# A round trip through DRAM in a Fourier and soft-MoE kernel: the transposing step moved from the reads to the stores, three weight tiles loaded earlier

## The chip, the cores and the metric

The kernel runs on one core of one Trainium2 chip, with its five engines: TensorE (PE), VectorE (DVE), ScalarE (ACT), GpSimd (POOL) and SyncE (SP), which issues nearly all transfers, in a fixed order. The metric is the device time of one execution in microseconds; lower is better.

## What is computed

The input x has 8 batches of 2,496 tokens with 256 channels. The first half is a spectral layer, the second a soft mixture of 8 experts with 4 slots each:

```python
X = rfft(x, axis=1)
Yr = Xr @ w_r - Xi @ w_i + b_r ; Yi = Xr @ w_i + Xi @ w_r + b_i
Y = softshrink(Yr, 0.01) + 1j * softshrink(Yi, 0.01)
x = irfft(Y).reshape(19968, 256)

logits = x @ phi                       # 32 columns
d = softmax(logits over all tokens)    # per slot
slot_out[e] = relu((d.T @ x)[e] @ w1[e]) @ w2[e]
c = softmax(logits over the 32 slots)  # per token
out = c @ slot_out
```

## The kernel before, in words

A transform of length 2,496 is done as 39 x 64: with `f1` over 39 points, then over 64. The token index is split so that each half is a matrix product on TensorE; between the halves the data has to be regrouped from "one partition per (position, frequency k)" to "one partition per position of the other factor", and this goes through DRAM. `a_unit` (L322) does the first half of a batch, writes its result `ast` to DRAM as `adr` and `load_ap` (L383) reads it back as `ap`. A step (`steps`, five per batch, four frequencies each) then does the second half (`f2`: px), the complex linear layer in split precision (`lin_k`: pk; `lin_y`: py), the shrinking (`rt`), the 32 logit columns of the spectrum (`tp_p`: pq, collected per batch as `p_sb`) and a transposed copy of the spectrum (`tp_t`: pt, T).

When the five steps of a batch are through, `c_stages` (L604) runs that batch's chain on the logits, beside the steps of the next batch: `p_sb` times `sinv` (pg) gives `g_sb`, the inverse transform over 64; `g_sb` is stored in DRAM as `gd`, read back as `gp` in another grouping, and `gp` times `m2` (pL) gives the logits `L` of the batch's tokens. From `L` follow the running maximum, the exponentials `ee`, a forward transform of them (`ea`, stored as `ed`, read back as `eb`), and the sums pr of the slots. `halves` (L578) splits each operand into a high and a low part: ScalarE casts `chpL` from `gp`, VectorE subtracts to get `clpL`, and three products make one. For batch 6 the operands are used unsplit. Batch 7 has no next batch: `last_chain` (L924) runs it in the tail, with `g_sb` stored in three parts (frequencies 0 to 11, 12 to 15, 16 to 19) as they come. Then the experts (hps, po) and the output (pq, ost, out).

Shapes of the regrouping: `g_sb` has 128 partitions, 2 parts c (real, imaginary) x 64 positions n, each with 20 frequencies k x 32 columns s. `gp` has 120 partitions, 3 groups r x 40 (c, k), each with 22 positions g x 32. Position n is 22r + g for the groups 0 and 1 and for g under 20 in group 2; its last two columns repeat positions 44 and 45, the first two of the same group.

The order of work is written out by hand. Each generator (`c_stages`, `a_unit`, `load_w` by `at` and so on) yields times of a made-up clock; a heap (`run_until`) records the instructions in the order of these times, and `_InOrder`, `sp`, `aq`, `mm` keep that order on every engine. A step is 4 units long, and TB = 166 is the time at which the steps end. The table `PLAN` holds the times: `pg`, `pL` and so on for the chain, `wl` for the 32 weight tiles (0.5 MB each, counted from TB, with a letter for the place: r, a, x and T reuse tiles of the chain or of the steps, x and T as two halves; t lies in a pool of NTA tiles, the second number of `nw`, that takes the place of the first half's buffers; h in a pool of the tail). The helper lines that the profile shows are L177 (all VectorE, ScalarE and GpSimd work), L234 (SP's transfers), L240 (products) and L530 (transposes).

Of the kernel before, what the change touches and what calls it, by code (L numbers as in the profile page):

```python
# [11 lines left out]
F32 = mybir.dt.float32  # L12
# [37 lines left out]
def _constants():  # L50
    n1 = np.arange(N1)
    k1 = np.arange(K1)
    a39 = 2 * np.pi * (np.outer(n1, k1) % N1) / N1
    c39, s39 = np.cos(a39), np.sin(a39)
    s39[:, 0] = 0.0
    a64 = 2 * np.pi * (np.outer(np.arange(N2), np.arange(N2)) % N2) / N2
    q = np.outer(np.arange(N2), np.arange(N2)) % N2
    c64, s64 = np.cos(a64), np.sin(a64)
    c64[(q == 16) | (q == 48)] = 0.0
    s64[(q == 0) | (q == 32)] = 0.0  # L60

    f1 = np.zeros((R, N1, R, 2, K1))
    m2 = np.zeros((R, 2, K1, R, N1))
    wk = np.where(k1 == 0, 1.0, 2.0) / N
    for r in range(R):
        f1[r, :, r, 0] = c39
        f1[r, :, r, 1] = -s39
        m2[r, 0, :, r] = (c39 * wk).T
        m2[r, 1, :, r] = (-s39 * wk).T
    f1 = f1.reshape(P1, Q1)  # L70
    m2 = m2.reshape(Q1, P1)

    suni = np.zeros((2, N2, 2, N2))
# [14 lines left out]
    smov = smov.reshape(128, K1 + 1, 64)
    smov = np.concatenate([smov[:, : KG + 1], smov[:, :1], smov[:, KG + 1 :]], axis=1).reshape(128, -1)
    sinv = suni[np.arange(128).reshape(2, N2).T.reshape(-1)].T  # L90
    sgn = np.ones((2, N2, K1))
    sgn[1] = sig.T
    sgn = sgn.reshape(128, K1)
    dsc = sgn * wk[None, :]

    ident = np.eye(128)
    dmask = np.tile(np.eye(32), (4, 4))
    f1a = f1.reshape(P1, R, 2, NGRP, KG).transpose(0, 3, 2, 4, 1).reshape(P1, Q1)
    f1 = f1.reshape(P1, R, 2 * K1).transpose(0, 2, 1).reshape(P1, Q1)
# [12 lines left out]
    return {k: np.ascontiguousarray(v.astype(np.float32)) for k, v in out.items()}
# [27 lines left out]
    "to": 0.7,  # L140
    "ws": [-29, -28.9, -28.8, 2],
    "late": {'6': {'cms': [19.75, 19.71, 860.75, 862, 864, 865], 'pd': [20.36, 20.37], 'pr': [31.55, 31.6, 31.65, 31.7, 31.75], 'pL': [5.4, 5.8], 'pm': 6.875, 'pb': 7.325, 'pe': [8.75, 9.75], 'pg': [0.875, 1.275], 'fr': {'sinv': 0, 'm2': 0, 'f1': 0, 'suni': 0}}, '5': {'pg': [1.1, 1.8], 'pL': [4.95, 5.75], 'pm': 6.8, 'pb': 7.15, 'pe': [9.2, 9.9], 'pd': [13.8, 14.8], 'pr': [15.0, 17.25, 19.5, 21.75, 24.0]}, '4': {'pr': [18.4, 20.49, 24.49, 28.49, 32.49]}},
    "T_": {'wl': [[-45, 'r'], [-44, 'r'], [-43, 'r'], [-31.0, 't'], [-30.7, 't'], [-29.4, 't'], [-27.6, 't'], [-27.8, 't'], [-11, 'a'], [-10.3, 'a'], [-9.6, 'a'], [-7.5, 'x'], [-6.4, 'x'], [1.11, 'x'], [1.07, 'h'], [1.08, 'h'], [1.09, 'h'], [1.1, 'h'], [1.11, 'h'], [13.55, 'h'], [13.1, 'h'], [13.6, 'h'], [13.6, 'h'], [13.61, 't'], [13.61, 't'], [13.61, 't'], [13.61, 't'], [13.61, 't'], [13.7, 'T'], [13.7, 'T'], [13.7, 'T'], [13.7, 'T']], 'cl': 16, 'cp': 46.5, 'ct': 46.6, 'du': [[-4.5, 0], [-2.4, 0], [1.2, 0]], 'd1': [5, 2, 4, 0, 0, 0], 'cm': [19.9, 19.91, 19.92, 25, 25.1, 25.2], 'cm7': [18, 20, 22, 23, 25, 27], 'ye': 0.2, 'te': [[5.6, 0.2], [5.5, 0.4]], 'pg': [-7, -3.25, -0.35], 'yt': 0.5, 'wr': -30.6, 'tp': [0, 0.9, 1.05, 0.5], 'tt': [[-0.4, 0.5, 0.6, 0.7, 0.8], [12, 12.1, 12.2, 12.3, 12.4]], 'z': 13.55, 'th': [0.1, 0.12], 'tl': [0.2, 0.25]},
    "f1": [1.5, 2.15],
    "kw": [[-40, 9]],
    "ap1": 1.85,
    "f0": 0.2,
    "nw": [3, 10, 9],
    "te": 'A',
    "tp": [0.5, 1.0, 1.9, 1.8],  # L150
    "tt": [2, 2.5],
# [29 lines left out]
def fourier_soft_moe_kernel(ctx: ExitStack, tc: tile.TileContext, t: dict, out: bass.AP):  # L181
# [396 lines left out]
    def halves(n, t0, times, out, const, fr, src, evac):  # L578
# [13 lines left out]
        for h in range(2):  # L592
# [8 lines left out]
            yield t0 + times[h] + 0.25  # L601
            evac(h, out[1](ps))

    def c_stages(b):  # L604
        ct_ = "ps"
        K_ = dict(PLAN, **PLAN["late"].get(str(b), {}))
# [8 lines left out]
            lambda h, ps: A.copy(out=g_sb[:, h * 10 : h * 10 + 10, :].rearrange("p k s -> p (k s)"), in_=ps),  # L615
        )
        yield t0 + K_["pg"][1] + 0.35
        gd = dr.tile([N2, 2 * K1, S], F32, tag="gd", name=f"gd{b}")
        sp(out=gd.rearrange("n (c k) s -> (n c) k s", c=2), in_=g_sb)
        yield t0 + K_["pg"][1] + 0.9  # L620
        gp = wtile([Q1, G, S], F32, "gp", f"gp{b}")
        for r in range(R):
            ge = 22 if r < 2 else 20
            p0 = r * 2 * K1
            sp(
                out=gp[p0 : p0 + 2 * K1, :ge, :],
                in_=gd[22 * r : 22 * r + ge].rearrange("g k s -> k g s"),
            )
# [295 lines left out]
    def last_chain():  # L924
        b = B - 1
        for (k0, k1), tk in zip(((0, 12), (12, 16), (16, 20)), T_["pg"]):
# [12 lines left out]
        for r in range(R):
            ge = 22 if r < 2 else 20  # L940
            p0 = r * 2 * K1
            sp(
                out=gp[p0 : p0 + 2 * K1, :ge, :],
                in_=gd[22 * r : 22 * r + ge].rearrange("g k s -> k g s"),
            )
            if ge < G:
                sp(
                    out=gp[p0 : p0 + 2 * K1, ge:, :],
                    in_=gd[22 * r : 22 * r + G - ge].rearrange("g k s -> k g s"),
                )  # L950
# [310 lines left out]
```

## Time and profile before

| | |
|---|---|
| median of 3 runs | 580.69 us (577.52 to 581.72) |
| profiled execution | 575.19 us, of which the span from first to last instruction is 573.4 us |
| mean granted TensorE clock | 0.971 |
| chain that ended last, by engine | PE 65%, DMA 14%, DVE 12%, ACT 3% |
| of it, DMA gp<-gd and gd<-g_sb | 3% and 3% |
| TensorE, VectorE, ScalarE, GpSimd busy | 92%, 73%, 52%, 49% |
| DMA moved | 118.55 MB, mean 207 GB/s |

How to read it: a timeline row has the start in us, the time that it took, engine, line, operation, tiles (out<-in), shape and how often; in brackets, how long the engine stood idle before and what ended that. SPq is SP's queue: such a row is the issue of a transfer, not the transfer. A row of the chain of waits has start, length and what it was; there a DMA is shown from the issue to the landing that somebody waited for. A row of the table of stretches has, per engine, busy us and instructions, then the granted TensorE clock, the mean busy share of the 16 DMA engines, and what they moved.

### The profile page before, as it was taken

The page shows a single profiled execution, that of the slowest core. Times are in us where ns is not written, and L with a number is a line of the kernel's source. Part 1 is how long each engine was busy: PE and PEld are TensorE (multiplying, and loading weights), DVE is VectorE, ACT ScalarE, POOL GpSimd, SP SyncE. Part 2 cuts the span into 40 slices and gives each one's busy share as a digit, 9 for nine tenths or more (in the row PEclk, how much of TensorE's full clock was granted, in tenths as well). Part 3 has the DMA queues.
Part 4 walks back from the last instruction along what each step waited for, and adds up shares of the span by engine and source line. Part 5 has one row for each costly group of instructions (what it writes and reads, how often), then busy time and mean ns, then how long its engine had stood idle before and what let it go on. Part 6 is the DMA issues. An engine that isn't in the chain of part 4 may idle for free.

```text
span 573.4 us, 11788 instructions
## 1 busy us (share of the span) xinstructions
PE 528.8 (92%) x4358; PEld 447.4 (78%) x4358; DVE 419.3 (73%) x837; ACT 298.6 (52%) x650; POOL 281.0 (49%) x258
## 2 busy tenths in 40 slices
PE   8668999999999999999999999998899989799894
PEld 4357999989898879889988888897687767367673
DVE  0254988789979897989689977986776764247783
ACT  4334555667566656665665656553333333037662
POOL 0035778667676666658655865773445412000100
PEclk9887999999999999999999999998989999999897
DMA  8779878667776858775787577866624489969898
GB/s 241 235 259 241 198 162 175 156 171 178 205 176 178 173 154 204 170 180 156 177 196 187 151 179 185 238 184 193 164 80 102 121 199 298 369 218 363 330 374 352
DMA packets 92884, 118.55 MB, mean 207 GB/s; under 512 B 46802, under 2 KB 68624, under 8 KB 92828
## 3 DMA queue, kind: packets, MB, share of 16 engines
q1 hardware_dynamic: 92572, 116.73, 73.0%
q10 hardware_dynamic: 256, 1.08, 0.5%
q8 instruction: 34, 0.56, 0.4%
q14 instruction: 22, 0.18, 0.1%
HBM read 68.42 MB, written 49.38 MB: 205 GB/s over the span
## 4 chain that ended last, share of the span: by engine, by line
PE 65%; DMA 14%; DVE 12%; ACT 3%; issue 2%; SPq 2%; POOL 0%; ACTq 0%; DVEq 0%; POOLq 0%
PE py L240 15%; PE px L240 10%; PE pq L240 8%; PE pk L240 7%; PE pa L240 7%; PE pt L530 4%; DMA gp<-gd 3%; DMA gd<-g_sb 3%; PE pr L240 3%; DMA ap<-adr 2%; SPq L234 2%; PE pc L1065 2%; DMA eb<-ed 2%; DMA xr<-in_x 2%; DVE mx L177 1%
## 5 line engine op out<-in xcount | busy, mean ns | idle before, releaser
L177 POOL TENSOR_TENSOR rt<-ut,rt 128x512 f32<-128x512 f32 x79 | 111.7, 1414 | 26.5 <-DVE rt L177 22.0
L177 POOL TENSOR_TENSOR xsl<-xsm,xsh 128x256 fp32r<-128x256 f32 x77 | 59.4, 772 | 107.3 <-DVE xsh L177 72.5
L177 POOL TENSOR_TENSOR xl<-xr,xh 117x512 fp32r<-117x512 f32 x73 | 98.4, 1349 | 21.8 <-ACT xh L177 13.8
L240 PE MATMUL px<-smov,ap 128*128 128x128 f32 x640 | 86.8, 280 | 5.7 <-DMA ap<-adr 3.9
L240 PEld LDWEIGHTS px<-smov,ap 128*128 128x128 f32 x640 | 81.5, 195 | 11.6 <-issue 4.7
L177 ACT COPY ast<-pa 120x512 f32<-120x512 f32 x86 | 50.6, 588 | 69.7 <-PE pa L240 68.1
L177 ACT CAST xth<-px 128x512 fp32r<-128x512 f32 x80 | 46.9, 586 | 74.0 <-PE py L240 38.2
L177 DVE SCALAR_TENSOR_TENSOR ut<-py,pk,k 128x256 f32<-128x256 f32 x160 | 69.5, 475 | 16.7 <-PE py L240 12.4
L177 DVE TENSOR_TENSOR xtl<-px,xth 128x512 fp32r<-128x512 f32 x80 | 54.6, 683 | 24.7 <-ACT xsm L177 22.6
L240 PE MATMUL py<-xth,nwsh 128*128 128x256 f32 x160 | 54.0, 337 | 0.0
L177 DVE TENSOR_SCALAR rt<-ut 128x512 f32<-128x512 f32 x69 | 53.3, 772 | 0.5
L240 PE MATMUL pk<-xsh,w_rh 128*128 128x256 f32 x160 | 49.3, 308 | 2.0 <-DVE xsh L177 2.0
L530 PE MATMUL pt<-pk,rt 128*128 128x128 f32 x320 | 45.9, 273 | 0.9 <-DVE dd L177 0.6
L177 ACT COPY T<-pt 128x512 f32<-128x512 f32 x70 | 42.0, 599 | 9.0 <-PE pt L530 7.0
L240 PE MATMUL pk<-xsl,w_rh 128*128 128x256 f32 x160 | 46.2, 289 | 0.0
L240 PE MATMUL pk<-xsh,w_rl 128*128 128x256 f32 x160 | 46.1, 288 | 0.0
L240 PE MATMUL py<-xtl,wdh 128*128 128x256 f32 x160 | 45.3, 283 | 0.0
L240 PE MATMUL py<-xth,wdl 128*128 128x256 f32 x160 | 45.2, 283 | 0.0
L240 PE MATMUL py<-xth,nwsl 128*128 128x256 f32 x160 | 45.2, 283 | 0.0
L240 PE MATMUL py<-xth,wdh 128*128 128x256 f32 x160 | 45.2, 282 | 0.0
L240 PE MATMUL py<-xtl,nwsh 128*128 128x256 f32 x160 | 45.1, 282 | 0.0
L240 PE MATMUL pq<-rhs,ct 128*128 128x512 f32 x156 | 43.1, 416 | 0.3 <-DVE ost L177 0.3
(186 smaller groups left out, 1245.8 us busy)
## 6 DMA issues: line engine op xcount, KB each, us to landing
ap<-adr SPq DMA_DIRECT2D x76, 256.0 KB
out<-ost SPq DMA_DIRECT2D x37, 512.0 KB
xr<-in_x SPq DMA_DIRECT2D x35, 480.0 KB
adr<-ast SPq DMA_DIRECT2D x20, 720.0 KB
w<-in_moe_w SPq DMA_DIRECT2D x25, 512.0 KB
adr<-ast SPq DMA_DIRECT2D x8, 480.0 KB
w<-in_moe_w SPq DMA_DIRECT2D x14, 256.0 KB
x<-in_x SPq DMA_DIRECT2D x11, 240.0 KB
```

Of the source, the lines that this page charges most:

```text
L177: return lambda *a, **k: self.tc.keep_in_program_order(f(*a, **k))
L234: tc.keep_in_program_order(nc.sync.dma_start(**kw))
L240: tc.keep_in_program_order(nc.tensor.matmul(**kw))
L530: tc.keep_in_program_order(nc.tensor.transpose(out=out, in_=in_, identity=identity))
L1065: nc.tensor.transpose(out=pc[:, i * P1 : (i + 1) * P1], in_=chls[b][x][:, 2 * (r + i) : 2 * (r + i) + 2].rearrange("p g h s -> p (g h s)") ...
```

## The change

The store and the reads between `g_sb` and `gp` are turned round. Before, each of the 128 partitions wrote its 20 x 32 values as one row of 2,560 bytes, and four reads per batch picked rows of 128 bytes. Now `gd` is ordered (c, k, n, s): two stores per batch, one for each c, write rows of 128 bytes (64 partitions x 20), and two reads take whole rows, 80 of 2,816 bytes for the groups 0 and 1 (two halves of 40 DRAM rows) and 40 of 2,560 for group 2. The last two columns of group 2 are copied on ScalarE (`gp_wrap`). So that these reads fall on neighbouring partitions, group 2 comes first in `gp` and `m2`, and the positions in `g_sb` are ordered with c outermost (`sinv`). In the last chain each of the three parts is stored in two.

The weights: of the 32 tiles, three more lie in the pool t, issued at TB-24, -22 and -20; the two that were issued at TB-7.5 and -6.4 into xth and xtl are gone from there, and the list behind is filled in again. The pool t gets 13 tiles instead of 10; the room comes from the scratch space that the program reserves for transfers, now 1,024 bytes.

```diff
-    m2 = m2.reshape(Q1, P1)
+    m2 = m2[[2, 0, 1]].reshape(Q1, P1)
...
-    sinv = suni[np.arange(128).reshape(2, N2).T.reshape(-1)].T
+    sinv = suni.T
...
-    "T_": {'wl': [..., [-31.0, 't'], [-30.7, 't'], [-29.4, 't'], [-27.6, 't'], [-27.8, 't'], [-11, 'a'], [-10.3, 'a'], [-9.6, 'a'], [-7.5, 'x'], [-6.4, 'x'], [1.11, 'x'], [1.07, 'h'], ...
+    "T_": {'wl': [..., [-31.0, 't'], [-30.7, 't'], [-29.4, 't'], [-27.8, 't'], [-27.6, 't'], [-24, 't'], [-22, 't'], [-20, 't'], [-11, 'a'], [-10.3, 'a'], [-9.6, 'a'], [1.07, 'h'], ..., [1.12, 'x'], [1.13, 'x'], [13.55, 'x'], ...
-    "nw": [3, 10, 9],
+    "nw": [3, 13, 9],
...
+    def gd_write(gd, g_sb, k0, k1):
+        for c in range(2):
+            sp(out=gd[c, k0:k1].rearrange("k n s -> n k s"), in_=g_sb[c * N2 : c * N2 + N2, k0:k1, :])
+
+    def gp_read(gp, gd):
+        rows = gd.rearrange("c k n s -> (c k) (n s)")
+        q = 2 * K1
+        sp(
+            out=gp[q:].rearrange("p g s -> p (g s)"),
+            in_=rows[:, : 2 * G * S].rearrange("q (r x) -> r q x", r=2),
+        )
+        sp(out=gp[:q, : G - 2, :].rearrange("p g s -> p (g s)"), in_=rows[:, 2 * G * S :])
+
+    def gp_wrap(gp):
+        A.copy(out=gp[: 2 * K1, G - 2 :, :], in_=gp[: 2 * K1, :2, :])
...
-        gd = dr.tile([N2, 2 * K1, S], F32, tag="gd", name=f"gd{b}")
-        sp(out=gd.rearrange("n (c k) s -> (n c) k s", c=2), in_=g_sb)
+        gd = dr.tile([2, K1, N2, S], F32, tag="gd", name=f"gd{b}")
+        gd_write(gd, g_sb, 0, K1)
...
-        for r in range(R):
-            ge = 22 if r < 2 else 20
-            p0 = r * 2 * K1
-            sp(
-                out=gp[p0 : p0 + 2 * K1, :ge, :],
-                in_=gd[22 * r : 22 * r + ge].rearrange("g k s -> k g s"),
-            )
-            if ge < G:
-                sp(
-                    out=gp[p0 : p0 + 2 * K1, ge:, :],
-                    in_=gd[22 * r : 22 * r + G - ge].rearrange("g k s -> k g s"),
-                )
+        gp_read(gp, gd)
         L = wtile([P1, G, S], F32, "L", f"L{b}")
+        yield t0 + K_["pL"][0] - PLAN["cl"][0] - 0.01
+        gp_wrap(gp)
...
-    nc = _bacc.Bacc("TRN2", target_bir_lowering=False, num_devices=1)
+    nc = _bacc.Bacc("TRN2", target_bir_lowering=False, num_devices=1, dynamic_dma_scratch_size=1024)
```

The same replacement stands in `last_chain`, with `gd_write(gd, g_sb, k0, k1)` for each part and `gp_wrap` just ahead of pL.

How it moves instructions: SP's queue around the chain of batch 0, before (the numbers behind the names tell tiles apart; the shape is that of the destination):

```order
L234 DMA gd_1290<-g_sb_1178 128x640
L234 DMA ap_4_1315<-adr_182 64x4x256 x2
L234 DMA gp_1326<-gd_1290 40x22x32 x2
L234 DMA gp_1326<-gd_1290 40x20x32
L234 DMA gp_1326<-gd_1290 40x2x32
L234 DMA xr_4_1332<-in_x 120x1024
L234 DMA adr_601<-ast_18_1295 120x1024
```

and now:

```order
L234 DMA gd_1290<-g_sb_1178 64x20x32 x2
L234 DMA ap_4_1316<-adr_182 64x4x256 x2
L234 DMA gp_1327<-gd_1290 80x1x704
L234 DMA gp_1327<-gd_1290 40x640
L234 DMA xr_4_1331<-in_x 120x1024
L234 DMA adr_601<-ast_18_1296 120x1024
```

One store has become two and four reads have become two; the neighbours are the same. ScalarE at the same place now, with the copy ahead of the two splits of `gp`:

```order
L177 COPY ast_0_1394<-pa_0_1395 120x512
L177 COPY gp_1327<-gp_1327 40x64
L177 CAST chpL_0_1405<-gp_1327 120x352
L177 CAST chpL_1_1421<-gp_1327 120x352
L177 CAST xth_4_0_1438<-px_4_0_1415 128x512
L177 COPY xsm_4_0_1440<-px_4_0_1415 128x256
```

The second row is new, the rest stands as before. SP's queue from the eb reads of batch 6 to those of batch 7 (w is a weight tile, w_0 and w_1 two halves of one), before:

```order
L234 DMA w_0_6425<-in_moe_w 128x512
L234 DMA w_1_6426<-in_moe_w 128x512
L234 DMA gd_6432<-g_sb_6431 128x384
L234 DMA w_0_6439<-in_moe_w 128x512
L234 DMA w_1_6440<-in_moe_w 128x512
L234 DMA gd_6432<-g_sb_6431 128x128 x2
L234 DMA gp_6540<-gd_6432 40x22x32 x2
L234 DMA gp_6540<-gd_6432 40x20x32
L234 DMA gp_6540<-gd_6432 40x2x32
L234 DMA w_6547<-in_moe_w 128x1024
```

and now:

```order
L234 DMA gd_6434<-g_sb_6433 64x12x32 x2
L234 DMA gd_6434<-g_sb_6433 64x4x32 x4
L234 DMA gp_6541<-gd_6434 80x1x704
L234 DMA gp_6541<-gd_6434 40x640
L234 DMA w_6546<-in_moe_w 128x1024
```

The two weight tiles between the stores are gone. Behind the reads there stood six tiles ahead of ed and one between ed and eb; now seven stand ahead of ed and none between. After eb there were 12 and are 11. The three tiles at TB-24, -22 and -20 now stand between the ap loads of batch 7's steps, two ahead of the store c_dr of batch 5 and one ahead of the gd stores of batch 6. On TensorE, VectorE and GpSimd the order is unchanged.

More of the change, by code (lines that the diff above doesn't have):

```diff
@@ L142 @@
     "late": {'6': {'cms': [19.75, 19.71, 860.75, 862, 864, 865], 'pd': [20.36, 20.37], 'pr': [31.55, 31.6, 31.65, 31.7, 31.75], 'pL': [5.4, 5.8], 'pm': 6.875, 'pb': 7.325, 'pe': [8.75, 9.75], 'pg': [0.875, 1.275], 'fr': {'sinv': 0, 'm2': 0, 'f1': 0, 'suni': 0}}, '5': {'pg': [1.1, 1.8], 'pL': [4.95, 5.75], 'pm': 6.8, 'pb': 7.15, 'pe': [9.2, 9.9], 'pd': [13.8, 14.8], 'pr': [15.0, 17.25, 19.5, 21.75, 24.0]}, '4': {'pr': [18.4, 20.49, 24.49, 28.49, 32.49]}},
-    "T_": {'wl': [[-45, 'r'], [-44, 'r'], [-43, 'r'], [-31.0, 't'], [-30.7, 't'], [-29.4, 't'], [-27.6, 't'], [-27.8, 't'], [-11, 'a'], [-10.3, 'a'], [-9.6, 'a'], [-7.5, 'x'], [-6.4, 'x'], [1.11, 'x'], [1.07, 'h'], [1.08, 'h'], [1.09, 'h'], [1.1, 'h'], [1.11, 'h'], [13.55, 'h'], [13.1, 'h'], [13.6, 'h'], [13.6, 'h'], [13.61, 't'], [13.61, 't'], [13.61, 't'], [13.61, 't'], [13.61, 't'], [13.7, 'T'], [13.7, 'T'], [13.7, 'T'], [13.7, 'T']], 'cl': 16, 'cp': 46.5, 'ct': 46.6, 'du': [[-4.5, 0], [-2.4, 0], [1.2, 0]], 'd1': [5, 2, 4, 0, 0, 0], 'cm': [19.9, 19.91, 19.92, 25, 25.1, 25.2], 'cm7': [18, 20, 22, 23, 25, 27], 'ye': 0.2, 'te': [[5.6, 0.2], [5.5, 0.4]], 'pg': [-7, -3.25, -0.35], 'yt': 0.5, 'wr': -30.6, 'tp': [0, 0.9, 1.05, 0.5], 'tt': [[-0.4, 0.5, 0.6, 0.7, 0.8], [12, 12.1, 12.2, 12.3, 12.4]], 'z': 13.55, 'th': [0.1, 0.12], 'tl': [0.2, 0.25]},
+    "T_": {'wl': [[-45, 'r'], [-44, 'r'], [-43, 'r'], [-31.0, 't'], [-30.7, 't'], [-29.4, 't'], [-27.8, 't'], [-27.6, 't'], [-24, 't'], [-22, 't'], [-20, 't'], [-11, 'a'], [-10.3, 'a'], [-9.6, 'a'], [1.07, 'h'], [1.08, 'h'], [1.09, 'h'], [1.1, 'h'], [1.11, 'h'], [1.12, 'x'], [1.13, 'x'], [13.55, 'x'], [13.6, 'h'], [13.6, 'h'], [13.6, 'h'], [13.6, 'h'], [13.61, 't'], [13.61, 't'], [13.61, 't'], [13.61, 't'], [13.61, 't'], [13.7, 'T']], 'cl': 16, 'cp': 46.5, 'ct': 46.6, 'du': [[-4.5, 0], [-2.4, 0], [1.2, 0]], 'd1': [5, 2, 4, 0, 0, 0], 'cm': [19.9, 19.91, 19.92, 25, 25.1, 25.2], 'cm7': [18, 20, 22, 23, 25, 27], 'ye': 0.2, 'te': [[5.6, 0.2], [5.5, 0.4]], 'pg': [-7, -3.25, -0.35], 'yt': 0.5, 'wr': -30.6, 'tp': [0, 0.9, 1.05, 0.5], 'tt': [[-0.4, 0.5, 0.6, 0.7, 0.8], [12, 12.1, 12.2, 12.3, 12.4]], 'z': 13.55, 'th': [0.1, 0.12], 'tl': [0.2, 0.25]},
     "f1": [1.5, 2.15],
@@ L931, in last_chain @@
                 g_sb = wtile([128, K1, S], F32, "g7", f"g_sb{b}")
-                gd = dr.tile([N2, 2 * K1, S], F32, tag="gd", name=f"gd{b}")
+                gd = dr.tile([2, K1, N2, S], F32, tag="gd", name=f"gd{b}")
             ps = psum("pf", f"pg{b}_{k0}")
@@ L935, in last_chain @@
             A.copy(out=g_sb[:, ks, :].rearrange("p k s -> p (k s)"), in_=ps[:, :n])
-            sp(out=gd.rearrange("n (c k) s -> (n c) k s", c=2)[:, ks, :], in_=g_sb[:, ks, :])
+            gd_write(gd, g_sb, k0, k1)
         yield TB + 1
         gp = wtile([Q1, G, S], F32, "gp", f"gp{b}")
[L939 to L950, printed above, removed]
+        gp_read(gp, gd)
         L = wtile([P1, G, S], F32, "L", f"L{b}")
         mx = wtile([P1, 4, S], F32, "mx", f"mx{b}")
+        yield TB + 6.9
+        gp_wrap(gp)
         yield TB + 7
```

## The prediction

> **What bounds the kernel now.** I read the page first, then busy time by stage, then the places where the chain under change meets TensorE.
>
> ```profile
> PE 528.8 (92%) x4358; PEld 447.4 (78%) x4358; DVE 419.3 (73%) x837; ACT 298.6 (52%) x650; POOL 281.0 (49%) x258
> ...
> DMA packets 92884, 118.55 MB, mean 207 GB/s; under 512 B 46802, under 2 KB 68624, under 8 KB 92828
> ```
>
> ```profile
> core 0: us, PE busy (x) PEld busy (x) DVE busy (x) ACT busy (x) POOL busy (x), PEclk, DMA share, GB/s
> 100.00:380.00 280.00, 274.35 (x2457) 246.38 (x2456) 241.43 (x480) 172.79 (x380) 187.47 (x162) 1.00 0.72 180
> 412.00:436.00 24.00, 22.10 (x178) 18.52 (x182) 17.25 (x37) 7.26 (x19) 10.64 (x11) 0.86 0.44 122
> 441.40:442.40 1.00, 1.00 (x12) 0.59 (x13) 0.46 (x2) 0.00 (x0) 0.61 (x1) 1.00 0.87 136
> 476.00:479.00 3.00, 2.46 (x16) 2.08 (x17) 1.69 (x6) 0.82 (x2) 0.00 (x0) 1.00 0.97 392
> 490.40:512.00 21.60, 20.85 (x254) 9.98 (x254) 5.72 (x18) 3.86 (x12) 0.00 (x0) 1.00 0.95 345
> ```
>
> From 100 to 380 us (the chains of batches 0 to 4) TensorE is busy for 274.35 of 280 us: there a wait of TensorE is lost and a shorter chain wins nothing. Now that chain in batch 0, by the timelines of SP, ScalarE, VectorE and TensorE:
>
> ```profile
> 107.23 0.35 SPq L234 DMA_DIRECT2D gd<-g_sb  x1
> 107.68 1.97 SPq L234 DMA_DIRECT2D ap<-adr  x2
> 111.23 3.32 SPq L234 DMA_DIRECT2D gp<-gd  x4
> ```
>
> ```profile
> 116.31 0.88 ACT L177 CAST chpL<-gp 120x352 fp32r<-120x352 f32 x2 [0.82 <-DMA gp<-gd]
> ```
>
> ```profile
> 116.83 2.10 DVE L177 TENSOR_TENSOR clpL<-gp,chpL 120x352 fp32r<-120x352 f32 x2 [0.95 <-ACT chpL L177]
> ```
>
> ```profile
> 117.93 0.41 PE L240 MATMUL pL<-chpL,m2h 120*117 120x352 f32 x1
> ...
> 118.34 0.32 PE L240 MATMUL pL<-clpL,m2h 120*117 120x352 f32 x1
> ```
>
> ```profile
> 283.38 0.18 PEld L240 LDWEIGHTS pL<-clpL,m2h 120*117 120x117 f32 x1 [0.27 <-DVE clpL L177]
> ```
>
> ```profile
> L177 DVE TENSOR_TENSOR clpL<-gp,chpL x12: 510/611/1614, 116.8 to 391.1; 120x352 fp32r<-120x352 f32 x12
> ```
>
> The reads land 5.08 us after their first issue (111.23 to 116.31). The first split is done at 116.8 and TensorE wants it at 117.93: 1.1 us to spare. The low half (510 to 1614 ns; the pair took 2.10, so the first is near one end or the other) is wanted at 118.34: between 1.0 us to spare and none; in batch 3 (the row at 283.38) TensorE already waits 0.27. I take 0.6 to spare.
>
> In batches 5, 6 and 7 the chain does set the time:
>
> ```profile
> 380.90 0.35 SPq L234 DMA_DIRECT2D gd<-g_sb  x1
> 381.31 0.42 SPq L234 DMA_DIRECT2D adr<-ast  x1
> 383.15 4.83 SPq L234 DMA_DIRECT2D gp<-gd  x4
> ...
> 436.45 0.34 SPq L234 DMA_DIRECT2D gd<-g_sb  x1
> 439.78 2.67 SPq L234 DMA_DIRECT2D gp<-gd  x4
> 442.54 1.25 SPq L234 DMA_DIRECT2D ap<-adr  x2
> ...
> 459.90 1.39 SPq L234 DMA_DIRECT2D eb<-ed  x2
> 461.39 1.42 SPq L234 DMA_DIRECT2D w<-in_moe_w  x2
> ...
> 468.41 2.85 SPq L234 DMA_DIRECT2D gp<-gd  x4
> ```
>
> ```profile
> 390.63 0.64 PE L240 MATMUL pL<-chpL,m2h 120*117 120x352 f32 x1 [2.38 <-ACT chpL L177]
> ...
> 444.43 0.82 PE L240 MATMUL pL<-gp,pk 120*117 120x352 f32 x2
> 445.79 0.85 PE L240 MATMUL pL<-gp,pk 120*117 120x352 f32 x2 [0.54 <-ACT L L177]
> ...
> 447.33 1.13 PE L240 MATMUL px<-smov,ap 128*128 128x128 f32 x8 [0.58 <-DMA ap<-adr]
> ```
>
> ```profile
> 465.53 2.80 DMA gd<-g_sb
> ...
> 469.38 3.87 DMA gp<-gd
> 473.38 1.41 PE pL L240 x4
> ...
> 484.62 5.61 DMA eb<-ed
> ```
>
> Batch 5 costs TensorE 2.38 us. In batch 6 the ap loads stand behind the reads in SP's queue. In batch 7 store and reads are links of the chain that ended last.
>
> **Prices.** One DMA engine moves 392 / (0.97 x 16) = 25.3 GB/s (476 to 479 us, weights). From 441.4 to 442.4 little but 128-byte rows is in flight: 136 GB/s are 1,062 rows in 1 us, and 0.87 x 16 engine-us over 1,062 is 13.1 ns a row. The store of batch 5 lands in 2.25 us (380.90 to 383.15); its eight 2,560-byte rows on each engine are 0.81 us of that, so 1.43 us is fixed.
>
> **Over how many engines a DMA is spread.** Take from the 46,802 packets under 512 bytes the gp and eb reads (8 x 2,640 + 8 x 2,560 = 41,600) and the 117 rows of f1a: 5,085 remain. The program has 340 DMAs: 195 with 64 or 128 rows, 90 with 120, 32 with 40 (the gp reads), 19 with 117, 4 with 72. The largest divisors up to 16 are 16, 15, 10, 13 and 12, and 195 x 16 + 90 x 15 + 32 x 10 + 19 x 13 + 4 x 12 = 5,085: one small packet for each engine of each DMA. So the old reads ran on 10 engines each. All 340 have the same outermost count on both sides. The new first read has not: 80 partitions in SBUF, in DRAM two halves of 40 rows (the listing's 80x1x704). If it is cut where both sides can be cut, it gets two engines; if the 80 alone decide, 16. I take two, since in all 340 the number divides both counts.
>
> [...] The 5,085 agree with the divisor; that both sides count, no run here shows. [...]
>
> **The change part by part.**
>
> Stores. Instead of 128 rows of 2,560 bytes, 2 x 1,280 of 128 bytes: 160 on each engine, 160 x 13.1 = 2.1 us instead of 0.81, so it lands 1.3 us later. The second issue (eb<-ed, the same shape read, takes 1.39 for two) lies within that. No 128-byte store is in the trace; bounds: nothing, if the store waits for engines anyway (batch 0 took 4.00, 107.23 to 111.23, against 2.25 in batch 5), and twice the read's price, +3.4. I take 1.3, as the next fixed price is that of a row of this size.
>
> Reads. The first: 40 rows of 2,816 bytes on each of two engines, 40 x 2,816 / 25.3 = 4.45, with 1.43 fixed 5.9 us: 0.8 more than 5.08. The second (ten engines, four rows of 2,560 each, issued 0.35 later) lands after 2.2. Bounds of the pair: 2.2 (16 engines, 0.56 us of rows) and 7 if the two engines also have older work.
>
> The copy on ScalarE waits for the second read alone, so it lies under the first, which is 3.7 us later, and costs nothing; without that cover it is one small copy on the path, 0.3 us by the nearest row, the copy of lg:
>
> ```profile
> L177 ACT COPY lg<-pq 128x128 f32<-128x128 f32 x39 | 10.7, 273 | 11.4 <-PE pq L240 11.4
> ```
>
> Behind it on ScalarE stand chpL and then the xth and xsm of the next step, for which VectorE waits: they come late with chpL, by the same amount as TensorE.
>
> *Batches 0 to 4:* the reads land 1.3 + 0.8 = 2.1 us later, 0.6 is to spare, TensorE loses 1.5 each: +7.5 (1.0 each with 1.1 to spare, 2.1 with none).
>
> *Batch 5:* nothing to spare; +2.1.
>
> *Batch 6:* the store lands at 441.1, the reads at 447.0. The ap loads are issued 0.7 earlier, but on two engines stand behind the rows. TensorE's first pL moves from 444.43 to 447.1; from there to px are 2.9 us, of which 0.58 was the wait for ap, so px starts at 449.4: +2.1.
>
> *Batch 7:* the last quarter goes in 2 stores of 256 rows: 0.35 + 1.43 + 0.2 = 2.0 to 2.2 us, not 2.80, as the weights that were issued at 461.39 are gone from there: -0.6. Reads 5.9 against 4.84 (468.41 to 473.25): +1.1. Then eb: seven weight tiles instead of six stand before ed, on two engines starting later; the tile between ed and eb is gone (0.5 MB, 1.3 us): they cancel, 0 within 1.3. Together +0.5.
>
> *Weights:* three tiles move to 412 to 436 us, where the engines are busy at 0.44 and SP issues little: 0 (if an ap load meets one, 1.3). After eb one tile fewer is loaded; from 490.4 to 512 TensorE is busy for 20.85 of 21.6 us, so that wins nothing. The scratch only makes room.
>
> Sum: 7.5 + 2.1 + 2.1 + 0.5 = +12.2 us on the profiled execution's 575.19. That execution lies 5.5 below the median of the three runs, so I put the change on the median: 580.69 + 12.2 = 592.9; its own range, from the ends of the loop's and the tail's terms, is 586 to 598.
>
> **Rivals.**
>
> *The first read runs on 16 engines* (faster). The reads then land 2.5 us after the issue with the copy behind them, 2.6 earlier than now; with the store's 1.3 the chain is 1.3 shorter. Batches 0 to 4 win only batch 3's 0.27, batch 5 1.3, batch 6 its wait for ap (0.6), batch 7 0.6 + 2.3 and about 1.0 at eb: -6.1, 574.6. For it: the engines of all other DMAs follow their 64 to 128 partitions. Against: two DRAM halves. It decides as soon as the first read lands in less than 3 us.
>
> *The store costs no more*, since its rows wait behind older ones anyway. Lateness 0.8 per batch, 0.2 after the spare time: 5 x 0.2 + 0.8 + 0.8 + 0.5 = +3.1, 583.8. For it: batch 0's 4.00 us. Against: on the engine that is free last, 160 rows still follow.
>
> [...]
>
> **How the numbers follow.** Chances: the forecast 0.43, 16 engines 0.25, the store for nothing 0.20, the double store 0.12. 1% (5.8 us) is about what a measurement of this kernel can tell. Faster by more: somewhat over half of the second, 0.15. Within 1%: the rest of it and the third, 0.29. Slower: 0.56. The range 573 to 601 leaves out the lower part of the second case and most of the last, under 0.2.
>
> **What would show it.** Right: the first gp read lands about 6 us after its issue and the second far earlier; packets under 512 bytes fall to 46,050 (40,960 rows of 128 bytes, 117 of f1a, and 4,973 small ones, counted as above; with 16 engines for the first read 46,162); ScalarE waits 2 us and more for gp in batches 0 to 5; TensorE shows gaps ahead of pL and is busy for less than 98% from 100 to 380 us; gd lands 1.3 us later. Wrong: reads of 2 to 3 us (then the first rival), a store that lands as before (the second), or TensorE without gaps at pL although gp is late, so that the time to spare was larger than read here.

## The result, and the profile after

The change takes 622.62 us (median of 4 runs, 621.14 to 626.89) against 579.28 for the kernel before on the same chip (4 runs, 577.52 to 581.72): 43.3 us more. The ratio on record is 1.080, 95% interval 1.0746 to 1.0853 (the two medians alone give 1.075). The forecast was 592.9 us, its range ended at 601: slower was right, the size was wrong by more than a factor of three. The profiled execution has a span of 624.9 us (573.4 before) and took 626.89. The two traces thus lie 51.5 us apart, more than the medians; sums that are taken from the traces below explain the 51.5.

The page of the change: busy time, packets, and the chain that ended last by engine and by line.

```profile
PE 542.9 (87%) x4358; PEld 458.0 (73%) x4358; DVE 412.3 (66%) x837; ACT 299.0 (48%) x658; POOL 279.4 (45%) x258
...
DMA packets 91428, 118.47 MB, mean 190 GB/s; under 512 B 46050, under 2 KB 67488, under 8 KB 91372
...
PE 59%; DMA 22%; DVE 8%; ACT 4%; issue 3%; SPq 2%; POOL 1%; ACTq 0%; POOLq 0%
PE py L240 14%; DMA gp<-gd 10%; PE px L240 9%; PE pq L240 7%; DMA gd<-g_sb 6%; PE pa L240 6%; PE pk L240 5%; PE pt L530 3%; PE pL L240 3%; PE pr L240 3%; SPq L234 2%; DMA ad<-ast 2%; PE pc L1063 2%; DMA eb<-ed 1%; PE pe L240 1%
```

The packets under 512 bytes are exactly the 46,050 that were forecast for a first read on two engines (46,162 for 16). In the chain that ended last the reads of gp have grown from 3% to 10%, the stores of gd from 3% to 6%. TensorE runs the same 4,358 products and is busy 14.1 us longer with them (528.8 before): those products took longer each, which is the first sign of something that the forecast did not have.

The chain of batch 0, by the timelines of SP and of ScalarE:

```profile
109.77 1.81 SPq L234 DMA_DIRECT2D gd<-g_sb  x2
111.67 2.13 SPq L234 DMA_DIRECT2D ap<-adr  x2
114.67 1.18 SPq L234 DMA_DIRECT2D gp<-gd  x2
115.95 0.34 SPq L234 DMA_DIRECT2D xr<-in_x  x1
116.39 0.36 SPq L234 DMA_DIRECT2D adr<-ast  x1
...
471.24 1.40 SPq L234 DMA_DIRECT2D gd<-g_sb  x2
476.70 1.17 SPq L234 DMA_DIRECT2D gp<-gd  x2
```

```profile
123.08 0.24 ACT L177 COPY gp<-gp 40x64 f32<-40x64 f32 x1 [5.04 <-DMA gp<-gd]
123.23 0.87 ACT L177 CAST chpL<-gp 120x352 fp32r<-120x352 f32 x2
```

From the store's issue to the reads' issue are 4.90 us (109.77 to 114.67; 4.00 before), from the reads' issue to the cast 8.56 (5.08 before). From batch 0 to batch 4 the store takes 0.9 to 2.5 us longer than before (1.5 in the mean), in batch 5 5.23 instead of 2.25 and in batch 6 5.46 instead of 3.33. What this does to TensorE, by its timeline at the first pL of batches 0 to 7 (in brackets the time that it stood idle before):

```profile
123.76 0.64 PE L240 MATMUL pL<-chpL,m2h 120*117 120x352 f32 x1 [3.05 <-ACT chpL L177]
...
181.45 0.64 PE L240 MATMUL pL<-chpL,m2h 120*117 120x352 f32 x1 [2.59 <-ACT chpL L177]
...
242.30 0.42 PE L240 MATMUL pL<-chpL,m2h 120*117 120x352 f32 x1 [3.44 <-ACT chpL L177]
...
302.70 0.64 PE L240 MATMUL pL<-chpL,m2h 120*117 120x352 f32 x1 [3.86 <-ACT chpL L177]
...
364.93 0.43 PE L240 MATMUL pL<-chpL,m2h 120*117 120x352 f32 x1 [4.24 <-ACT chpL L177]
...
424.27 0.64 PE L240 MATMUL pL<-chpL,m2h 120*117 120x352 f32 x1 [7.42 <-ACT chpL L177]
...
487.12 1.49 PE L240 MATMUL pL<-gp,pk 120*117 120x352 f32 x2 [7.98 <-DMA gp<-gd]
...
523.54 2.67 PE L240 MATMUL pL<-gp,pk 120*117 120x352 f32 x4 [7.08 <-DMA gp<-gd]
```

These are 39.7 us of waits; before, TensorE's products stood waiting at the same places for 2.38 in batch 5, for 2.37 in batch 7 (below) and not at all elsewhere.

```profile
473.38 1.41 PE L240 MATMUL pL<-gp,pk 120*117 120x352 f32 x4 [2.37 <-DMA gp<-gd]
```

That is 35 us of a difference of 51.5 between the two spans. The rest stands in the column PEclk of the table of stretches, here around the wait of batch 0 in the change:

```profile
116.00:123.00 7.00, 4.71 (x38) 4.27 (x37) 2.30 (x6) 1.32 (x4) 3.20 (x3) 1.00 0.66 184
123.40:126.70 3.30, 2.94 (x12) 2.85 (x13) 2.93 (x7) 3.23 (x8) 1.29 (x2) 0.50 0.06 25
127.00:134.00 7.00, 6.93 (x62) 5.83 (x61) 6.03 (x13) 3.28 (x7) 2.98 (x4) 1.00 0.62 146
```

Behind the wait, TensorE's granted clock is 0.50 for 3.3 us: 12 products in a stretch that at full clock holds more than twice as many (62 in 7 us, the row below). The trace has such a stretch at every one of the eight waits, 3.41 us or a multiple of it up to 13.65 (by batch 3.41, 3.41, 3.41, 6.83, 3.41, 10.24, 13.65 and 10.24). It begins 2.0 us (batch 3) to 5.0 us (batch 4) after the wait did, in six of the eight within the wait. With two more behind shorter waits the stretches between 48 and 560 us add up to 61.4 us, against 13.65 before. Of the 47.8 us more, some 16 lie inside the waits and cost nothing further (4.0, 5.4 and 4.2 of them in batches 5 to 7); the other 32 are worth 16 us at half speed, an estimate. TensorE's busy time, which needs no such estimate, has grown by 14.1 us and its idle time by 37.4 (82.0 instead of 44.6); 35 of these 37.4 lie at pL. Together that is the 51.5. The shortest of the eight waits, 2.59 us (batch 1), was enough for a stretch of 3.41; why the stretches are that long is not shown.

### The profile page after: what moved, and what is told of

It reads as the page before. It is cut to its first block, busy times and chain, and to the rows that moved or that the text cites. A ratio compares the mean times of both kernels' runs of the same rounds, so it can differ in the third digit from the quotient of the medians.

```text
span 624.9 us, 11776 instructions
## 1 busy us (share of the span) xinstructions
PE 542.9 (87%) x4358; PEld 458.0 (73%) x4358; DVE 412.3 (66%) x837; ACT 299.0 (48%) x658; POOL 279.4 (45%) x258
## 2 busy tenths in 40 slices
DMA packets 91428, 118.47 MB, mean 190 GB/s; under 512 B 46050, under 2 KB 67488, under 8 KB 91372
## 4 chain that ended last, share of the span: by engine, by line
PE 59%; DMA 22%; DVE 8%; ACT 4%; issue 3%; SPq 2%; POOL 1%; ACTq 0%; POOLq 0%
PE py L240 14%; DMA gp<-gd 10%; PE px L240 9%; PE pq L240 7%; DMA gd<-g_sb 6%; PE pa L240 6%; PE pk L240 5%; PE pt L530 3%; PE pL L240 3%; PE pr L240 3%; SPq L234 2%; DMA ad<-ast 2%; PE pc L1063 2%; DMA eb<-ed 1%; PE pe L240 1%
## 5 line engine op out<-in xcount | busy, mean ns | idle before, releaser
L240 PE MATMUL px<-smov,ap 128*128 128x128 f32 x640 | 88.6, 284 | 9.1 <-DMA ap<-adr 5.8
L240 PEld LDWEIGHTS px<-smov,ap 128*128 128x128 f32 x640 | 83.2, 198 | 15.2 <-issue 9.3
L177 DVE TENSOR_SCALAR rt<-ut 128x512 f32<-128x512 f32 x69 | 52.0, 754 | 0.5
L177 ACT COPY T<-pt 128x512 f32<-128x512 f32 x70 | 41.8, 597 | 10.2 <-PE pt L530 7.0
```

What stands on the lines that cost most here:

```text
L177: return lambda *a, **k: self.tc.keep_in_program_order(f(*a, **k))
L240: tc.keep_in_program_order(nc.tensor.matmul(**kw))
```

## The experiments

**Theory A:** the first read lies on two DMA engines, and this makes TensorE wait; each wait is paid twice, once as idle time and once at half clock behind it. **Rivals:** the time goes into the store, the weight tiles or the on-chip copy; or the lower clock is a by-product that costs nothing. Each ratio below is against the kernel before on the same chip (medians 576.29 to 577.85 there).

### The 80 rows as two reads of 40

```diff
-        sp(out=gp[q:]..., in_=rows[:, : 2 * G * S].rearrange("q (r x) -> r q x", r=2))
+        for r in range(2):
+            sp(out=gp[q + q * r : 2 * q + q * r].rearrange("p g s -> p (g s)"), in_=rows[:, r * G * S : (r + 1) * G * S])
```

> The 80-row read is made as two reads of 40 rows (one DRAM half each), so that both sides of every gp read have the outermost count 40; stores, copy and weights are those of the change. Theory A (the read that runs on two DMA engines is the cause, and TensorE's half clock after each wait makes it larger): the reads land in about 3.3 us instead of 8.4 (12 rows of 2,816 or 2,560 bytes on each of ten engines, 1.3 us, behind 1.5 us to the first row and 0.5 to the landing), the waits ahead of pL in batches 0 to 4 go, and the time is 572 to 580 us. Rival B (the 128-byte stores, or the longer chain of store, read and copy as such, are the cause): 600 us or more.

583.15 us, ratio 1.0108 (1.0056 to 1.0160). The page and SP's timeline of this variant:

```profile
DMA packets 91572, 118.47 MB, mean 204 GB/s; under 512 B 46194, under 2 KB 67632, under 8 KB 91516
```

```profile
107.91 1.80 SPq L234 DMA_DIRECT2D gd<-g_sb  x2
109.80 2.21 SPq L234 DMA_DIRECT2D ap<-adr  x2
112.78 1.03 SPq L234 DMA_DIRECT2D gp<-gd  x3
```

The small packets rise by 144 = 8 x (10 + 10 - 2): each half-read runs on ten engines. The last of the 80 rows comes 3.35 us after the first issue in batch 0, where it came after 7.5. Of 8.0% more only 1.1% is left, but the expected 572 to 580 us were missed: it stays above the kernel before.

### The 80 rows as two reads by columns, still on two engines

```diff
+        for h in range(2):
+            x = slice(h * 11 * S, h * 11 * S + 11 * S)
+            sp(out=gp[q:]...[:, x], in_=rows[:, : 2 * G * S].rearrange("q (r x) -> r q x", r=2)[:, :, x])
```

> The control to it: the 80-row read is also made as two reads, but cut along the columns, 80 rows of 1,408 bytes each, so that the DRAM side still has the outermost count 2. Theory A: each runs on the same two engines with the same bytes, the reads land in about 8.5 to 9 us, 620 to 630 us. Rival (one long transfer, or rows of 2,816 bytes, are what is slow, not the two engines): clearly under 610 us.

622.02 us, ratio 1.0787 (1.0735 to 1.0839): nothing changes, and the small packets rise by 16 = 8 x 2 to 46,066. That there are two reads is not what helps.

### One read, its source rows outermost

```diff
-    m2 = m2[[2, 0, 1]].reshape(Q1, P1)
+    m2 = m2.reshape(R, 2 * K1, P1)
+    m2 = np.concatenate([m2[2], m2[:2].transpose(1, 0, 2).reshape(4 * K1, P1)])
...
-            in_=rows[:, : 2 * G * S].rearrange("q (r x) -> r q x", r=2),
+            in_=rows[:, : 2 * G * S].rearrange("q (r x) -> q r x", r=2),
```

> The change, with one thing turned: the read of 80 rows of 2,816 B runs over its 40 source rows outermost and the two groups within, so that its two nested loops begin at 80 on chip and 40 in DRAM instead of 80 and 2; the rows land in another order on chip and the constant m2 is reordered to match. Same bytes, same 80 rows, still one DMA, same store. Theory A (two DMA engines carry the read because of the 2 that stands outermost in DRAM): the read's rows spread over more engines, it lands 4 us or more sooner, ACT's waits on gp fall from 51 to under 20 us, and the time is 578 to 586 us, as with two reads of 40 rows. Theory B (two reads of 40 rows were faster because they were two DMAs, or because of the row order): 610 us or more.

585.38 us, ratio 1.0186 (1.0157 to 1.0214). The page, and ScalarE's timeline in batch 0:

```profile
DMA packets 91492, 118.47 MB, mean 204 GB/s; under 512 B 46114, under 2 KB 67552, under 8 KB 91436
```

```profile
118.67 0.24 ACT L178 COPY gp<-gp 40x64 f32<-40x64 f32 x1 [1.79 <-DMA gp<-gd]
```

64 more small packets are 8 x (10 - 2): the same DMA of the same 80 rows now runs on ten engines. The reads' issue (113.49) to the copy takes 5.18 us instead of 8.41, with ScalarE waiting 1.79 instead of 5.04. Only the order of two loops has changed (and, to match, that of the rows on chip and in `m2`); this shows the two engines as the cause of most of the loss. By the small packets (46,050, 46,194, 46,114) outermost counts of 80 and 2, 40 and 40, 80 and 40 went with 2, 10 and 10 engines; each of these numbers divides both counts.

### Products in the waits

The second theory, that the half clock costs time of its own, is tried by keeping TensorE at work while it waits: products of the unit matrix into an unused accumulator, just ahead of the first pL.

```diff
+        step_to(warm_up(t0 + K_["pL"][0] - 0.001, 26 if b < 5 else 60))
...
+    def warm_up(t, n):
+        yield t
+        dummy(n)
```

(and `dummy(60)` ahead of pL in `last_chain`)

> The changed kernel with products of the identity that nobody reads, ahead of the first pL of each batch (26 for batches 0 to 4, 60 for 5 to 7; 0.11 us each), so that TensorE has work while it waits for gp. They leave all results as they are. If the half clock after the waits is a part of the loss (theory A: waits 35 us longer than before, and some 16 us by the clock): the waits stay, the granted clock goes back to about 0.97 and the time falls by 10 to 16 us, to about 608. If the waits alone are the loss: 622 us or more.

636.68 us, ratio 1.1035 (1.0985 to 1.1084): slower, because the filler was twice as long as meant. The timeline of this variant shows two products for each call, 52 and 120 in place of 26 and 60:

```profile
117.72 5.97 PE L240 MATMUL dps<-pk 128*128 128x128 f32 x52
...
418.03 13.66 PE L240 MATMUL dps<-pk 128*128 128x128 f32 x120
```

5 x 5.97 + 3 x 13.66 = 70.8 us of filler overrun 39.7 us of waits by 31, yet the time rises by only 14, a first sign that something was won back. The test was repeated with half the filler (13 and 30 calls).

> The change with products of the unit matrix into an unused accumulator ahead of each first pL matmul, 13 calls (26 passes, about 3.0 us) in batches 0 to 4 and 30 calls (60 passes, about 6.8 us) in batches 5 to 7: half of what the earlier filler had, so that it fits inside the waits instead of overrunning them. The result of the kernel is not touched. Theory A (the two-engine read makes TensorE wait 2.6 to 8 us ahead of each pL, and each such wait is followed by a stretch of half clock that costs as much again): the waits stay as waits, now filled with products, the half-clock stretches behind them go, and of the 61 us at half clock in the change (some 24 us of lost time beyond what the kernel before loses with its 14 us at half clock) 10 to 17 us come back: 605 to 613 us, mean granted clock at 0.97 or more. Theory B (the lower clock is a by-product that costs nothing, since the vector engines and transfers set the pace by then): 620 us or more.

608.11 us, ratio 1.0567 (1.0536 to 1.0598): 14.5 us less than the change by the medians, 13.5 by the ratios, as expected. The stretch behind the wait of batch 0 and the filler in it:

```profile
123.30:126.70 3.40, 3.40 (x22) 2.98 (x23) 3.37 (x8) 3.29 (x8) 1.79 (x2) 1.00 0.10 23
```

```profile
119.82 3.07 PE L240 MATMUL dps<-pk 128*128 128x128 f32 x26
...
123.26 0.42 PE L240 MATMUL pL<-chpL,m2h 120*117 120x352 f32 x1 [0.38 <-ACT chpL L177]
```

22 products in 3.4 us at full clock, where the change did 12 in 3.3; pL starts no earlier, since it still waits for gp. The half clock is a cost of its own: about 14 us, where TensorE's busy time gave 14.1 and the stretches outside the waits 16.

### The weight list alone, and the rest without the store and the row reads

First the kernel before with the weight list, the 13 tiles and the small scratch, and nothing else:

```diff
-    "nw": [3, 10, 9],
+    "nw": [3, 13, 9],
...
-    nc = _bacc.Bacc("TRN2", target_bir_lowering=False, num_devices=1)
+    nc = _bacc.Bacc("TRN2", target_bir_lowering=False, num_devices=1, dynamic_dma_scratch_size=1024)
```

(with the change's list `wl`)

> The kernel before with the new list of weight times, 13 tiles in the pool and the scratch of 1,024 bytes, but with its own store and reads. Theory A: the weights are no part of the loss; the two half tiles are gone from the last chain, 574 to 580 us against 579.3. Rival (the moved weights or the tail's new order cost a part): 585 us or more.

576.1 us (10 runs), ratio 0.9964 (0.9931 to 0.9996): no part of the loss. Then the change with the old store and the old layout of gd, the three large reads of before, and the on-chip copy for the fourth:

```diff
+        for p0, g0, ge in ((0, 44, G - 2), (q, 0, G), (2 * q, 22, G)):
+            sp(out=gp[p0 : p0 + q, :ge, :], in_=gd[g0 : g0 + ge].rearrange("g k s -> k g s"))
...
+        gd = dr.tile([N2, 2 * K1, S], F32, tag="gd", name=f"gd{b}")
+        sp(out=gd.rearrange("n (c k) s -> (n c) k s", c=2), in_=g_sb)
```

> The store and DRAM layout of the kernel before (one DMA, 128 rows, 2,560 B each, over all queues), the three reads of 128-B pieces of the kernel before without its fourth, small one (40 x 2 x 32), and in its place the on-chip copy of two columns; weights list and DMA scratch as in the change. So of the change only the two separate stores and the whole-row reads are undone. Theory A (the store in 128-B rows to two stores costs some 1 us of issue and 1 to 2 us of landing in the batches where TensorE waits, the two-engine read the rest): 572 to 578 us, level with or a little under the kernel before, and 5 to 10 us under the variant with two 40-row reads. Theory B (the on-chip copy with its wait on ACT costs as much as the small read saves, or more): 580 us or more.

574.8 us (10 runs), ratio 0.9966 (0.9934 to 0.9999), as theory A had it and the same as with the weight list alone: copy and weights together cost nothing. Its median is 8 to 11 us below those of the two variants whose whole-row read runs on ten engines; these differ from it in the store and in the reads' shape, so this is the loss that is left when the two engines are repaired. SP's timelines put most of it on the store. In batch 6 store to reads is 439.83 to 445.48 = 5.65 us with the two stores and 439.30 to 441.61 = 2.31 with one:

```profile
439.83 1.40 SPq L235 DMA_DIRECT2D gd<-g_sb  x2
...
445.48 1.37 SPq L235 DMA_DIRECT2D gp<-gd  x2
```

```profile
439.30 0.33 SPq L234 DMA_DIRECT2D gd<-g_sb  x1
...
441.61 1.69 SPq L234 DMA_DIRECT2D gp<-gd  x3
```

(first the variant with source rows outermost, then the one with three reads).

### Smaller terms: four tests, none of which moved the time

*The second store on another queue* (from the variant with source rows outermost):

```diff
-            sp(out=gd[c, k0:k1]...
+            (sp, aq)[c](out=gd[c, k0:k1]...
```

> The variant whose large read runs over 40 source rows outermost (585.4 us), with the second of the two stores issued by ACT's queue beside SP's instead of behind the first on SP's. Theory A (of the 2.6 to 3.3 us by which the two stores are slower than the one of before in batches 5 and 6, about half is that the second is issued only when the first has been, 0.7 to 0.9 us apart, and the rest that 2,560 rows of 128 B take longer than 128 rows of 2,560 B): gp's reads are issued 0.5 to 1 us earlier in each batch, 579 to 583 us. Theory B (the rows alone take the time, the second store waits for nothing): within 2 us of 585.

586.57 us, ratio 1.0148 (1.0109 to 1.0186), against 1.0186 without: no difference that can be measured; theory A fell.

```profile
441.62 0.60 SPq L235 DMA_DIRECT2D gd<-g_sb  x1
441.63 0.63 ACTq L238 DMA_DIRECT2D gd<-g_sb  x1
```

The two stores are now issued at the same time, and the reads still follow 5.7 us later (447.33). In the trace the 2,560 rows run from 1.25 to 4.99 us after the issue, as they ran from 1.24 to 4.84 with one queue. In both, 95% of the rows are through 2.4 us after the first began, some 15 ns a row if each of 16 engines has 160 of them. The reads of eb (as many rows of the same size, batch 6 of the kernel before) have 95% through after 1.9 us and the last after 2.1. The store's last 5% take 1.2 to 1.4 us more, and the reads of gp wait for the last row. So the store costs its rows and a late end, and the second queue changed neither; what holds the last rows up is open.

*The load of x behind the reads moved away*, first 6 us later (`tu - 4` for `tu - 6`), then ahead of the store (`tu - 7.2`):

> The change with the one load of x that stands right behind gp's reads on SP's queue (120 rows of 4,096 B, batches 2 to 7) issued two planner units, about 6 us, later; all else as it is. Theory A (part of the read's 7.5 us, where 40 rows of 2,816 B on an engine would need 4.5 us, is time that the two engines give to the transfers issued right behind it, the load of x and the store of adr): the last row of gp comes 0.5 to 1 us earlier, waits ahead of pL in batches 0 to 4 fall by as much, 614 to 619 us. Theory B (the two engines are slow on their own, 147 ns a row whatever else runs): no change, 620 to 625 us.

620.45 us, ratio 1.0789 (1.0743 to 1.0836). This tested nothing: SP stood at the reads of gp until the store had landed, so the load came 0.44 us later and no more (116.39 instead of 115.95, only behind the store of adr now).

> The change with the load of x that stands right behind gp's reads on SP's queue put ahead of the store of gd instead (batches 2 to 7; 120 rows of 4,096 B): an earlier attempt to put it 6 us later moved it by 0.4 us alone, because SP's queue stood at the reads of gp anyway. The store of adr (120 rows of 4,096 B) stays behind the reads. Theory A (the two engines of the large read lose time to the transfers issued right behind it): with half of those rows gone the last row of gp comes 0.6 to 1.2 us after issue sooner (7.5 us in the change), if SP does not reach the store of gd later for it: 612 to 619 us. Theory B (the two engines are slow on their own): rows as late as before, 620 to 625 us.

623.51 us (median of three runs; a fourth took 629.26), ratio 1.0766 (1.0712 to 1.0819), no change in time. In the trace the last of the 80 rows comes 7.1 to 7.3 us after the issue in batches 0 to 4 instead of 7.5 to 7.7: the load of x accounts for 0.3 us, less than theory A asked for. Most rows took 112 ns, but in each batch single rows took 500 to 900; what holds these up is open.

*The small read first:*

```diff
-        sp(out=gp[q:]..., in_=rows[:, : 2 * G * S]...)
         sp(out=gp[:q, : G - 2, :]..., in_=rows[:, 2 * G * S :])
+        sp(out=gp[q:]..., in_=rows[:, : 2 * G * S]...)
```

> The change with its two reads issued in the other order: the 40 rows of 2,560 B first, the 80 rows of 2,816 B behind them. Same bytes, same engines, same copy. Theory A (in the change the small read cannot land early: 8 of its 40 rows go to the two engines that carry the large one and come only behind that one's rows, so the on-chip copy waits for both reads and stands in the path with 0.24 us and its own landing): issued first, its rows are there some 4 us ahead of the last row of the large read, the copy runs under that read, and each pL starts 0.3 to 0.7 us earlier, 614 to 620 us. Theory B (the copy was hidden, as the prediction had it): no change, 620 to 625 us, or slower, since the large read starts 0.6 us later.

622.31 us, ratio 1.0758 (1.0704 to 1.0812): no difference; theory A was right on the place of the copy and wrong on its worth. ScalarE's timeline in batch 0:

```profile
118.16 0.24 ACT L177 COPY gp<-gp 40x64 f32<-40x64 f32 x1
123.39 0.87 ACT L177 CAST chpL<-gp 120x352 fp32r<-120x352 f32 x2 [4.99 <-DMA gp<-gd]
```

The copy now runs 5 us ahead of the cast, while in the change it ran 0.15 us ahead of it. But the reads were issued at 114.95, so the cast comes 8.44 us behind them against 8.56: what the copy gives back, the large read loses by starting later on the same two engines.

### A kernel under both

The variant with three reads, with products in the two waits of batch 5 behind which it shows half clock:

```diff
+        if b == 5:
+            step_to(warm_up(t0 + K_["pL"][0] - 0.001, 11))
+            step_to(warm_up(t0 + K_["pd"][0] - 0.001, 9))
```

> The kernel with the store of before, its three large reads and the on-chip copy in place of the fourth (574.8 us), and in batch 5 alone products of the unit matrix into an unused accumulator in the two waits behind which its trace shows a stretch of half clock: 11 calls ahead of pL (wait 2.87 us, about 2.5 us filled) and 9 ahead of pd (2.37 us, about 2.0 us filled). Theory A (a wait of TensorE costs a second time, by the 3.41 us at half clock behind it): both stretches go, up to 3.4 us come back, 571 to 574 us, under the kernel before. Theory B (in batch 5 the transfers and the vector engines set the pace, not TensorE's clock): 574 to 577 us, the stretches gone or not.

572.9 us (6 runs), ratio 0.9897 (0.9857 to 0.9937): 1% below the kernel before and, by 50 us, below the change. Against the variant without these products (0.9966) the intervals just touch, so that part of the gain rests on the trace. The stretches of batch 5, without the products and with them:

```profile
380.00:400.00 20.00, 17.13 (x143) 15.22 (x132) 12.26 (x26) 8.88 (x22) 10.88 (x11) 0.91 0.58 146
400.00:425.00 25.00, 21.12 (x182) 18.87 (x180) 17.81 (x40) 9.74 (x23) 10.57 (x11) 0.93 0.80 213
```

```profile
380.00:400.00 20.00, 19.65 (x182) 17.79 (x175) 13.76 (x28) 10.11 (x24) 11.28 (x12) 1.00 0.66 165
400.00:425.00 25.00, 23.34 (x214) 20.34 (x213) 20.84 (x46) 9.11 (x22) 11.42 (x13) 1.00 0.78 207
```

Both stretches are at full clock, and VectorE, which had no products added, gets through 46 instructions instead of 40 in the second.

## Why the prediction was wrong in size

Right: the first read runs on two engines (46,050 packets, and the three read variants); the chain of gd and gp has little cover in the loop (1.3 us by the sum below) and none in batches 5 to 7; the weights cost nothing (0.9964). TensorE between 100 and 380 us is at

```profile
100.00:380.00 280.00, 258.97 (x2220) 232.59 (x2220) 214.91 (x437) 158.41 (x352) 169.74 (x147) 0.96 0.65 160
```

which is 92% where 98% stood, as the prediction's last part asked.

Wrong, step by step, with what each measured:

| step | predicted | measured |
|---|---|---|
| first read, from its issue | landed after 5.9 us | last row after 7.5 us (80 rows in 5.96 us on two engines, 149 ns each) |
| "The second (ten engines, ...) lands after 2.2" | 2.2 us | last rows at 7.8 us, behind the first read's |
| the copy "lies under the first ... and costs nothing" | 0 | behind both reads: cast 8.56 us after the issue, 5.08 before |
| store to reads | +1.3 | +0.9 to +2.5 in batches 0 to 4, +3.0 in batch 5, +2.1 in batch 6 |
| batches 0 to 4, TensorE's wait | 5 x 1.5 = 7.5 | 3.05 + 2.59 + 3.44 + 3.86 + 4.24 = 17.2 |
| batch 5, 6, 7 | 2.1, 2.1, 0.5 | 5.0, 8.0, 4.7 (7.42 - 2.38; 7.98; 7.08 - 2.37) |
| waits in all | 12.2 | 34.9 |
| half clock behind the waits | no term | 14.1 by TensorE's busy time, 13.5 to 14.5 by the filler of half size |

*The reads.* This term was mis-sized: 0.8 us later was counted, 3.5 later (8.56 - 5.08) was measured. The prediction took the pair as two independent transfers and gave each its bytes at the full rate. In batch 0 the 8.56 us from the issue to the cast are 1.53 to the first row, 5.96 for the 80 rows, 0.40 for the last rows of the other read, 0.52 from there until ScalarE goes on, and 0.15 for the copy; the forecast was 1.43 + 4.45. The pace is thus the largest part of the miss: 149 ns a row instead of 111, 1.5 us in all, of which the load of x explains a fifth (0.3). The fixed part was 0.6 too small. And eight of the second read's 40 rows come only when the first read's are through (7.4 to 7.9 us after the issue), as they would if four of them had gone to each of the same two engines; landing and copy follow. The swapped order shows that even the hidden copy wins nothing, which fits an end that is set by the sum of the rows on those two engines. The bound of 7 us for the pair "if the two engines also have older work" was on the page and still too low. With the store's 0.9 the chain of batch 0 is 4.4 us later where 2.1 was counted; less the 3.05 us wait, that leaves 1.3 to spare, so the cover of 0.6 was taken too small, and the lateness far too small.

*The store.* In size nearly right in the loop (1.5 in the mean, rising from 0.9 to 2.5), too small where nothing covers it: 3.0 and 2.1 in batches 5 and 6 against 1.3. The price came from reads of 128-byte rows (13.1 ns); 95% of the stored rows were through at 15 to 17 ns a row if each of 16 engines has 160 of them, and the last ones came up to 1.4 us behind the rest. No run shows a small store at twice the read's price, to which the prediction gives a chance of 0.12: that was +3.4 us by its bound, where the store came 0.9 to 3.0 later, and the runs give the store and the reads' shape together 8 to 11 us in all.

*The half clock.* This is the step that was missing, a term put at nothing without a reason. Its evidence stood in the profile of the kernel before: the table of stretches has a granted clock of 0.86 between 412 and 436 us, and the prediction quotes that row for its DMA share without asking why the clock is low. Batch 5's wait of 2.38 us had such a stretch behind it already. A wait that did not exist before was priced at its own length, while each of the eight in the change brought 3.41 us or more at half speed.

In the traces the terms add up: 34.9 of waits at pL and 14.1 of slower products are 49.0 of the 51.5 us between the spans, the other 2.5 idle time elsewhere. By parts of the change: with the read on ten engines 1.0108 and 1.0186 are left of 1.080, so the two engines (their half clock included) are 6 to 7%; the store in 128-byte rows with its whole-row reads is most of the rest; weights and copy are nothing.

Two small sums of the prediction do not come out as written: the ends that it names for its terms give 589 to 597 us where it has 586 to 598, and its chances add up to 0.30 within 1% and 0.55 slower where it has 0.29 and 0.56. The result lies far outside both ranges.

## What to carry to other kernels

Before a transfer is priced by its bytes, look at the outermost count on both of its sides: 80 and 2 gave two engines here (46,050 small packets), and turning the two loops gave ten for the same rows (46,114); and add up everything that is queued on those few engines, a second transfer's share too (eight of its 40 rows came 7.4 to 7.9 us after the issue). Where TensorE is nearly always busy (98% from 100 to 380 us before), price a new wait as the wait plus half of what the stretch at half clock reaches beyond its end: here waits of 2.59 to 7.98 us brought stretches of 3.41 to 13.65 us, and 34.9 us of new waits came with 14.1 of slower products. Products into an unused accumulator won 14.5 us back where they were about as long as the wait or shorter (608.11 for 622.62 us), and lost 14 where they were longer (636.68). Rows of 128 bytes took longer to store than to read here (2.7 to 3.9 us from the first to the last in batches 0 to 4 of the change, against 2.1 to 2.3 for as many rows read), so a transposition is not free to move from the read to the store.

## What the hardware showed that was not expected

- A wait of 2.59 us (batch 1 of the change) already brought TensorE's clock to one half, for 3.41 us; waits of 7 to 8 us brought 10.2 to 13.7 us. The length of a wait alone does not tell: in batch 5 of the kernel before, 1.79 us ahead of pd were followed by 6.83 us at half clock, while 3.08 us ahead of pd in batch 7 were followed by none. Between 48 and 560 us of the traces of the kernel before and of the change, all six waits of TensorE of more than 3.2 us had such a stretch, and so had seven of the nine between 1.6 and 3.2. In each of the two traces the stretches there begin and end whole multiples of 3.41 us apart (in the change the first begin at 123.35, 181.38 and 242.82 us: 58.03 and 61.44 are 17 and 18 times 3.413). What decides whether a wait has one, no run here shows.

```profile
413.14 0.41 PE L240 MATMUL pd<-chpd,sunih 128*128 128x320 f32 x1 [1.79 <-ACT chpd L177]
...
490.37 1.31 PE L240 MATMUL pd<-eb,pk 128*128 128x320 f32 x4 [3.08 <-DMA eb<-ed]
```

- 128-byte rows over 16 engines: in batches 0 to 4 of the change 2,560 of them read (eb) ran in 2.1 to 2.3 us, 2,560 stored (gd) in 2.7 to 3.9, with 13 ns in most rows' records in both cases (in batch 5 the read took 3.8 too). In batches 3 to 6 of the store the last 5% of the rows came 0.9 to 1.4 us behind the rest. Issuing the store from two queues at once changed nothing.
- A load that was placed some 6 us later in SP's program was issued 0.44 us later, since SP stood at a wait in between (116.39 instead of 115.95).
